# A first tile that is finished in PSUM, and a second MoE whose second layer streams tokens instead of weights

## The chip, the cores and the metric

One program runs on one NeuronCore of a Trainium2 chip. Its engines work beside each other and wait for one another through semaphores: TensorE (PE, matrix products into PSUM, which has eight banks of 512 fp32 a partition), VectorE (DVE), ScalarE (ACT), GpSimd (POOL) and SyncE (SP, which here only starts DMAs). The metric is device microseconds (us) of one execution, as the median of several; lower is better.

## The reference, cut to what matters

```python
# delta attention: q, k, v of shape (4, 8, 768, 48), one 48x48 state per head
for t in range(S):
    y[:, :, t] = q_t @ state
    state = state + bt * outer(kt, vt - kt @ state)
x = y.transpose(0, 2, 1, 3).reshape(3072, 384)
# first MoE: 384 -> 2048 -> 384
h = x @ w_in
x = (h * sigmoid(1.702 * h)) @ w_out
# second MoE: 4 experts, 384 -> 1024 -> 384
p = domain_probs / (domain_probs.sum(-1) + 1e-9)
out = sum(p[:, e:e+1] * (np.maximum(x @ w1[e], 0) @ w2[e]) for e in range(4))
```

Everything is fp32. A product of the MoEs is done as three products of parts: each operand is split into a high part and the rest, and high x high, high x rest and rest x high are added in PSUM (`PASSES`).

## The kernel before, in words

The 768 positions are twelve chunks of 64, called u = 0 to 11. Two chunks of all four batches are one tile of 512 tokens, so there are six tiles, t = 0 to 5.

**Attention.** For each chunk a chain of small fp32 products runs over the heads (each leaves two records in the trace): Gram matrices of the keys (L511, L514), products of keys and queries (L444), for u = 0 and 1 two more that complete an inverse (L661, L670), keys times state (L733), solves (L743, twice), a cross term (L753), the output `y` (function `read`, L765) and the state update (`write`, L770). Chunks 0 and 1 are worked in two halves of the heads, one after the other. `y` comes out with one head pair's 48 rows on partitions 0 to 47 and another's on 64 to 111. For the first MoE the 384 features must lie on 128 partitions in three parts, so `y_copy` moves three heads of four into the tile `stage` and the fourth into a side buffer `YS`, and six DMAs of 16 rows (`put`, L848) bring the pieces of the fourth head into the 16 free partitions under each 48. Then `split_stage` splits `stage` into the two parts that the MoE takes (`xs`, L180 and L878).

**First MoE.** A visit f of 16 takes 128 hidden features: nine products into `ph` (function `layer1`, L884: three parts of x, three passes), the gate on ACT and DVE, and nine products into the three `px` banks (L972) that are issued a visit late. In both layers the weights are loaded into the array and 512 tokens stream through it. Tile 0 does its first eight visits on 256 tokens of u = 0, then on 256 tokens of u = 1, then eight on all 512; tile 1 is worked in halves throughout. The weights of tile 0's visits are themselves split into parts on ACT and DVE shortly before they are used (`queue_w1`, L262 to L277).

**What sets the order.** `manual_schedule` keeps instructions as they are written. `Order` writes attention tasks into the stream of MoE products by a cost model with clocks, priorities and ready times; `until` moves its clock on until a task is done. Each engine then runs its own list in order, so a product that waits holds all later products.

**Second MoE.** For each expert e and tile t, eight visits f. Layer 1 is as before. ACT and DVE make the two parts of the hidden tile, `hh` (L1112, L1113). In `layer2_2` (L1086) the hidden tile is loaded into the array, 128 tokens at a time, and 384 columns of weights stream: twelve products for the four groups of tokens. After the eighth visit DVE scales each `po` bank by the tokens' probability and adds it to `oacc` (L1092, L1094); after the last expert a DMA writes each 128 tokens out (L1098). The part of x for the next tile is split during the visit before the last (L1077, L1078); the first one is split when the first MoE is over. The weights of the next expert are split in the last tile of an expert.

Of the kernel before, what the change touches and what calls it, by code (L numbers as in the profile page):

```python
# [149 lines left out]
def delta_attention_moe_moe_kernel(  # L150
# [17 lines left out]
    E = probs.shape[1]  # L168
    F2 = we.shape[0] // E
# [52 lines left out]

    def load_w2(n):
        nc.sync.dma_start(out=raw[:, n % 2, :], in_=we[n])

    def split_w2(n):
        t = wp.tile([128, 2, 768], F32R, name="w", tag="w")
        half = raw[:, n % 2, :]
# [94 lines left out]
    V = nc.vector  # L323

# [98 lines left out]
    def queue_q(u):  # L423
# [11 lines left out]
        for g0 in range(0, NP, 8):  # L435
            cell = {}

            def gram(g0=g0, cell=cell):
                ps = cell["ps"] = psa.tile([128, 8, C], F32, name="gp", tag=claim(BANKS, cell["end"]))
                for i in range(8):  # L440
                    g = g0 + i
                    for x in range(2):
                        d = DR[x]
                        mm(ps[TR[x]:TR[x] + C, i, :], lhsT=kt[d:d + D, g, :], rhs=pq[d:d + D, g, x, :],  # L444
                           start=True, stop=True)

            def mask(x, g0=g0, cell=cell):
                r = TR[x]
                V.tensor_tensor(out=pq[r:r + C, g0:g0 + 8, x, :], in0=cell["ps"][r:r + C],  # L449
                                in1=pmask[r:r + C].unsqueeze(1).broadcast_to([C, 8, C]), op=ALU.mult)  # L450

            visits.append(gram)
            masks += [(cell, lambda x=x, mask=mask: mask(x)) for x in range(2)]
            if len(visits) == whole:
                t = task(lambda fs=tuple(visits): [f() for f in fs], "PE", 1.0 * whole,
                         (*placed[u], lq, begun[0], *ends[-1:]), prio=p + 1, can=lambda: some_free(BANKS, whole))
                for c, f in masks:
                    c.setdefault("end", []).append(task(f, "DVE", 0.6, (t,), prio=p + 1))
                    ends.append(c["end"][-1])
                visits.clear()  # L460
                masks.clear()
# [225 lines left out]
    def queue_chain(u):  # L687
# [27 lines left out]
        for hu in range(2):  # L715
# [65 lines left out]
            def s_add(x, gs=gs, cell=cell):  # L781
# [4 lines left out]
                else:  # L786
# [3 lines left out]
                               read=read, write=write, y_copy=y_copy, s_add=s_add))  # L790


        for hs in [halves[0:1], halves[1:2]] if u < 2 else [halves]:
# [29 lines left out]
            if n == 1:  # L823
                h, = hs
                reads = [task(h["read"], "PE", 1.0, (*bs, pdone[u]), prio=p, can=lambda: free_at("yg"))]
# [4 lines left out]
            for h, y in zip(hs, reads):  # L830
                ye = h["cell"]["yev"] = [task(lambda e, x=x, h=h: h["y_copy"](e, x), ("ACT", "DVE"), (0.7, 0.72), (y,), prio=p,
                                              can=y_free) for x in range(2)]
                wr = task(h["write"], "PE", 0.82, bs, prio=p) if n == 1 else reads[0]
# [7 lines left out]


        ov = []
        for x in range(2):
            for kk in range(KD):
                def put(x=x, kk=kk):
                    d, n = DR[x] + 16 * kk, DR[x] + D
                    (nc.scalar if u < 2 and x else nc.sync).dma_start(out=xst[n:n + 16, kk, u % 2], in_=YS[u][d:d + 16])  # L848

                ov.append(task(put, "ACT" if u < 2 and x else "HW", 0.45, yev, lat=2.3, prio=p, slack=5))  # L850
# [5 lines left out]
    xst = stage.rearrange("p (k c b i) -> p k c b i", k=KD, b=B, c=2)  # L856

# [31 lines left out]
    with tc.manual_schedule():  # L889
# [6 lines left out]
        nc.gpsimd.memset(SU, 0.0)  # L896
        m2 = scr[2][:, 0:C]
# [33 lines left out]
        x1 = {}  # L931
        x1d = [drx.tile([128, KD, TT], F32, name=f"x1d{t}") for t in range(KEEP)]
# [4 lines left out]
        def queue_w2(n):  # L937
            e, f = divmod(n, F2)
            WE[e, f] = split_w2(n)
            if n + 2 < E * F2:  # L940
                load_w2(n + 2)

        def x1_out(t):
# [16 lines left out]
            return ev  # L960

# [44 lines left out]
        def split_stage(t, cs, us, fs):  # L1006
            if not us:
                return split
            until(*(ydone[u] for u in us))
            if cs.start == 0:  # L1010
# [10 lines left out]
        for n, (t, cs, us, fs) in enumerate(items):  # L1021
            if cs.start == 0 and fs[0] == 0 and t + 2 < NW:
                queue_tile(t + 2)
            for f in fs:
# [17 lines left out]
                if t == NW - 1 and 1 <= f <= F2:  # L1042
                    queue_w2(f - 1)
                if t == NW - 1 and f == F1 // 2:
                    nc.vector.tensor_reduce(out=ptmp, in_=pr, axis=mybir.AxisListType.X, op=ALU.add)
                    nc.vector.tensor_scalar(out=ptmp, in0=ptmp, scalar1=1e-9, scalar2=None, op0=ALU.add)
                    nc.vector.reciprocal(out=ptmp, in_=ptmp)
                    nc.vector.tensor_tensor(out=pr, in0=pr, in1=ptmp.unsqueeze(3).broadcast_to([128, B, NW, E]), op=ALU.mult)
            if t == NW - 2:
# [8 lines left out]
                oacc = big.tile([128, B, NW, DM], F32, name="oacc")  # L1058
                pr = big.tile([128, B, NW, E], F32, name="pr")
                ptmp = big.tile([128, B, NW], F32, name="ptmp")  # L1060
# [4 lines left out]
                nc.sync.dma_start(out=pr, in_=probs.rearrange("(b t p) e -> p b t e", b=B, p=128))  # L1065
# [8 lines left out]
        def split_now(n, t, kk):  # L1074
            s = (xs2 if n % 2 else xsp).tile([128, 2, TT], F32R, name="xs", tag="xs")
            src = x1[t][:, kk, :]
            nc.scalar.copy(out=s[:, 0, :], in_=src)  # L1077
            nc.vector.tensor_tensor(out=s[:, 1, :], in0=src, in1=s[:, 0, :].bitcast(F32), op=ALU.subtract)  # L1078
            return s

        def layer2_2(e, t, f, hh, w):
            for b in range(B):
                if f == 0:
                    po[b] = ps2.tile([128, DM], F32, name="po", tag="po", bufs=6)
                for i, (a, c) in enumerate(PASSES):
                    mm(po[b], lhsT=hh[:, a, b * 128:(b + 1) * 128], rhs=w[:, c, 384:768],  # L1086
                       start=f == 0 and i == 0, stop=f == F2 - 1 and i == 2)
                if f == F2 - 1:
                    acc = oacc[:, b, t, :]
                    p = pr[:, b, t, e:e + 1]  # L1090
                    if e == 0:
                        nc.vector.tensor_scalar(out=acc, in0=po[b], scalar1=p, scalar2=None, op0=ALU.mult)  # L1092
                    else:
                        nc.vector.scalar_tensor_tensor(out=acc, in0=po[b], scalar=p, in1=acc,  # L1094
                                                       op0=ALU.mult, op1=ALU.add)
                    if e == E - 1:
                        r0 = b * S + t * 128
                        nc.sync.dma_start(out=out[r0:r0 + 128, :], in_=acc)  # L1098
# [3 lines left out]
        xs = [split_now(0, 0, kk) for kk in range(KD)]  # L1102
        for n, (e, t) in enumerate(seq):
            nt = seq[n + 1][1] if n + 1 < len(seq) else None
            for f in range(F2):
# [9 lines left out]
                if pend:  # L1115
                    layer2_2(*pend)
# [5 lines left out]
            if e + 1 < E and t == NW - 1:  # L1122
                queue_w2((e + 1) * F2 + F2 - 1)
        layer2_2(*pend)


def lay_out(q, k, v, beta, moe_w_in, moe_w_out, moe2_domain_probs, moe2_w1, moe2_w2):
# [13 lines left out]

    qt = flat(q.reshape(B, M, 2, U, C, D).transpose(3, 2, 5, 0, 1, 4), U, 2, D, B * M, C)
# [12 lines left out]
    for kk in range(KD):  # L1155
        for x in range(2):
# [4 lines left out]
    we = np.concatenate([flat(w1, -1, 128, DM), moe2_w2.reshape(-1, 128, DM)], axis=2)  # L1161
    return {"q": qt, "k": tokens(k), "v": tokens(v), "beta": betas, "w": w,
            "probs": np.ascontiguousarray(moe2_domain_probs), "we": we}
# [20 lines left out]
```

## Time and profile before

| | us |
|---|---|
| median of three runs | 1480.54 (1479.08 to 1483.88) |
| the profiled execution | 1484.33 |
| its span, first to last instruction | 1482.6 |
| PE busy | 1420.4 (96% of the span) |
| DVE busy | 619.3 (42%) |
| ACT busy | 459.8 (31%) |
| POOL busy | 191.9 (13%) |

The span has four parts: attention ahead of any MoE (to 86.55 us), the first tiles, in which attention and the first MoE share PE, the first MoE alone, and from 676.30 us the second MoE. PE counts as busy while a product is anywhere in its pipeline, so a busy PE isn't at its peak: a row of the timeline gives when a run of products starts, and the distance from one start to the next is what the run takes. An engine's idle time counts only where PE waits for it.

### The profile page before, as it was taken

What the parts mean: (1) busy time and instruction counts of PE and PEld (TensorE: products, weight loads), DVE (VectorE), ACT (ScalarE), POOL (GpSimd) and SP (SyncE); (2) the same over time, 40 slices, a digit from 0 to 9 for tenths busy, and PEclk for the clock granted to TensorE, in tenths of its full rate; (3) what the DMA queues carried; (4) which work ended last, traced back from release to release, by engine and by line L of the source; (5) the groups of instructions that cost most, each with busy time, mean ns of one, the idle gap of its engine ahead of it and who ended that gap; (6) DMA issues with size and microseconds to landing.
All of it is one profiled execution on the core that took longest, in us unless ns stands there. A gap on an engine that the chain in (4) does not pass through costs nothing.

```text
span 1482.6 us, 30388 instructions
## 1 busy us (share of the span) xinstructions
PE 1420.4 (96%) x13552; PEld 1258.2 (85%) x13552; DVE 619.3 (42%) x1033; ACT 459.8 (31%) x866; POOL 191.9 (13%) x340
## 2 busy tenths in 40 slices
PE   3687999999999999999999999999999999999999
PEld 2677889998888788888999999999999999999998
DVE  6978756545473423332223242232433223423222
ACT  5554434445353233432111231121321112222111
POOL 2019550080260530000000000000000000000000
PEclk8588999999999999999999999999999999999999
DMA  9211021201201000410000020000200000100001
GB/s 316 115 27 36 2 74 34 62 22 26 49 23 37 15 33 8 142 52 1 0 1 0 10 77 0 1 0 1 64 22 0 1 0 22 43 22 22 22 22 43
DMA packets 41331, 53.71 MB, mean 36 GB/s; under 512 B 25712, under 2 KB 29936, under 8 KB 41200
## 3 DMA queue, kind: packets, MB, share of 16 engines
q1 hardware_dynamic: 41008, 51.67, 11.7%
q8 instruction: 106, 1.74, 0.5%
q14 instruction: 25, 0.20, 0.0%
q10 hardware_dynamic: 192, 0.10, 0.0%
HBM read 42.71 MB, written 7.86 MB: 34 GB/s over the span
## 4 chain that ended last, share of the span: by engine, by line
PE 90%; DVE 2%; DMA 1%; ACT 1%; SPq 0%; issue 0%; DVEq 0%
PE ph L884 40%; PE po L1086 27%; PE px L972 13%; PE ch L743 2%; PE gp L444 2%; PE ch L733 1%; PE y L765 1%; DMA pq<-in_q_dram 1%; PE ch L753 1%; PE ch L770 1%; PE gp L511 1%; SPq L848 0%; DVE w L277 0%; DVE gh L990 0%; DVE scr L479 0%
## 5 line engine op out<-in xcount | busy, mean ns | idle before, releaser
L884 PE MATMUL ph<-xs,w 128*128 128x512 f32 (+1 forms) x2808 | 664.8, 379 | 3.7 <-DVE x L180 2.4
L884 PEld LDWEIGHTS ph<-xs,w 128*128 128x128 f32 x2808 | 499.7, 190 | 90.3 <-issue 2.8
L1086 PE MATMUL po<-w,hh 128*128 128x384 f32 x2304 | 432.8, 336 | 0.0
L1086 PEld LDWEIGHTS po<-w,hh 128*128 128x128 f32 x2304 | 407.6, 188 | 17.1
L1113 DVE SCALAR_TENSOR_TENSOR hh<-ph,hh 128x512 fp32r<-128x512 f32 x192 | 132.9, 692 | 554.0 <-ACT hh L1112 554.0
L1112 ACT ACTIVATE hh<-ph 128x512 fp32r<-128x512 f32 x192 | 115.0, 599 | 632.3 <-PE ph L884 632.3
L972 PE MATMUL px<-gh,w 128*128 128x512 f32 (+1 forms) x1080 | 233.5, 356 | 0.6 <-DVE gh L990 0.4
L972 PEld LDWEIGHTS px<-gh,w 128*128 128x128 f32 x1080 | 178.5, 192 | 29.4 <-DVE gh L990 2.0
L990 DVE TENSOR_TENSOR gh<-ph,gh 128x512 fp32r<-128x512 f32 (+1 forms) x120 | 69.5, 579 | 147.7 <-ACT gh L989 146.9
L987 ACT ACTIVATE ph<-ph 128x512 f32<-128x512 f32 (+1 forms) x120 | 59.5, 496 | 207.8 <-PE ph L884 203.5
L569 POOL TENSOR_TENSOR scr<-scr,itmp 128x30 f32<-128x30 f32 (+9 forms) x150 | 89.4, 596 | 11.8
L567 POOL TENSOR_TENSOR itmp<-scr 128x30 f32<-128x30 f32 (+9 forms) x150 | 81.4, 543 | 11.4
L989 ACT CAST gh<-ph 128x512 fp32r<-128x512 f32 (+1 forms) x120 | 60.2, 502 | 3.8
L180 ACT COPY su<-ch 32x384 f32<-32x384 f32 x77 | 36.2, 471 | 49.6 <-PE ch L743 45.0
L444 PE MATMUL gp<-pq,kt 48*64 48x64 f32 x768 | 34.2, 254 | 18.1 <-DMA pq<-in_q_dram 9.5
L444 PEld LDWEIGHTS gp<-pq,kt 48*64 48x64 f32 x768 | 31.3, 166 | 21.4 <-issue 8.3
L1078 DVE TENSOR_TENSOR xs<-x,xs 128x512 fp32r<-128x512 f32 x72 | 45.3, 684 | 2.0 <-ACT xs L1077 2.0
L511 PE MATMUL gp<-kt 48*32 48x64 f32 x768 | 28.2, 231 | 17.0 <-ACT kt L180 16.2
L743 PEld LDWEIGHTS ch<-v,scr 32*32 32x32 f32 x1536 | 36.5, 110 | 7.8 <-issue 4.6
L511 PEld LDWEIGHTS gp<-kt 48*32 48x32 f32 x768 | 25.2, 116 | 20.8 <-ACT kt L180 17.6
L743 PE MATMUL ch<-v,scr 32*32 32x48 f32 x1536 | 40.4, 208 | 0.7 <-DVE pq L449 0.5
L180 ACT COPY kt<-scr 32x512 f32<-32x512 f32 (+1 forms) x60 | 37.0, 617 | 12.0 <-DVE scr L333 11.1
(106 smaller groups left out, 809.6 us busy)
## 6 DMA issues: line engine op xcount, KB each, us to landing
raw<-in_we_dram SPq DMA_DIRECT2D x32, 384.0 KB, 3.1
rw<-in_w_dram SPq DMA_DIRECT2D x14, 768.0 KB, 12.2
k<-in_k_dram SPq DMA_DIRECT2D x12, 384.0 KB, 5.1
pq<-in_q_dram SPq DMA_DIRECT2D x24, 192.0 KB, 4.5
v<-in_v_dram SPq DMA_DIRECT2D x12, 384.0 KB, 3.2
out_dram<-oacc SPq DMA_DIRECT2D x24, 192.0 KB, 1.9
x1d<-raw SPq DMA_DIRECT2D x12, 256.0 KB, 2.3
x<-x1d SPq DMA_DIRECT2D x4, 768.0 KB, 5.8
```

The costliest lines, as they stand in the source:

```text
L180: (nc.scalar.copy if e == "ACT" else nc.vector.tensor_copy)(out=out_, in_=in_)
L444: mm(ps[TR[x]:TR[x] + C, i, :], lhsT=kt[d:d + D, g, :], rhs=pq[d:d + D, g, x, :], start=True, stop=True)
L511: mm(ps[r:r + SB, i, :], lhsT=kt[d:d + D, g, 0:SB], rhs=kt[d:d + D, g, :], start=True, stop=True)
L567: E.tensor_tensor(out=tv, in0=x[:, j:j + 1, j + 1:].broadcast_to([128, m, r]), in1=x[:, 0:m, j:j + 1].broadcast_to([128, m, r]), op=ALU.mult)
L569: E.tensor_tensor(out=x[:, 0:m, j + 1:], in0=x[:, 0:m, j + 1:], in1=tv, op=ALU.add)
L743: mm(cell["ps"][r:r + 32, i, :], lhsT=Tb[u][r:r + 32, g, :], rhs=V2[u][r:r + 32, g, :], start=True, stop=True, tile_position=(r, r))
L884: mm(ps, lhsT=w[:, a, kk * 128:(kk + 1) * 128], rhs=xs[kk][:, b, cs], start=kk == 0 and i == 0, stop=kk == KD - 1 and i == 2)
L972: mm(px[d][:, cs], lhsT=w[:, a, 384 + d * 128:384 + (d + 1) * 128], rhs=gh[:, b, 0:cs.stop - cs.start], start=f == 0 and i == 0 and cs.sta ...
L990: a = task(lambda: nc.vector.tensor_tensor(out=lo, in0=ph, in1=hi.bitcast(F32), op=ALU.subtract), "DVE", 0.07 + 0.53 * c, (a,), **kw)
L1086: mm(po[b], lhsT=hh[:, a, b * 128:(b + 1) * 128], rhs=w[:, c, 384:768], start=f == 0 and i == 0, stop=f == F2 - 1 and i == 2)
L1112: nc.scalar.activation(out=hh[:, 0, :], in_=ph, func=AF.Relu)
L1113: nc.vector.scalar_tensor_tensor(out=hh[:, 1, :], in0=ph, scalar=0.0, in1=hh[:, 0, :].bitcast(F32), op0=ALU.max, op1=ALU.subtract)
```

## The change

Three things are changed, and some tables around them.

**First tile.** For u = 0 and 1, `read` no longer makes the fourth head's outputs as 48 rows of their own. `S4`, a view of `stage`, is set to zero at the start on POOL; `fourth` copies the fourth head's 16 columns for each part beside zeros, so that a product with 64 columns of it puts them on rows 48 to 63 and zeros on the rows above, and the three-head product is added on top. The finished 128 rows are split straight from PSUM by `take_x` and `take_rest` into `xs0`. The copies, the six DMAs and `split_stage` are gone for tile 0. `write` now follows its half's `read`, and key and query products of u above 1 may only be placed once the first MoE has begun.

**Second MoE, layer 2.** In tiles 0 to 4 the weights are loaded and the 512 tokens of `hh` stream, into three banks of 128 features. The probabilities lie along the tokens then: they are normalised once, written to a DRAM buffer `prd`, and loaded per expert and tile, broadcast to all partitions, into half of `raw` (`load_pb`). DVE multiplies each bank by them and adds it. After the last expert DVE transposes blocks of 32x32 and sixteen DMAs write the tile out. The last tile keeps the old form (`layer2_last`), with its weight columns read in another order, since `lay_out` permutes them on the host. The next expert's weights are split in tiles 1 to 4, two a tile.

**First x of the second MoE.** `split_now(0, 0, kk)` is called four visits before the end of the first MoE.

```diff
-                    mm(py[o:o + D, i, :], lhsT=SU[:, c0:c0 + D], rhs=pq[:, g, x, :], start=True, stop=True)
+                    if not t and g % 4 == KD:
+                        continue
+                    if not t:
+                        g3 = g - g % 4 + KD
+                        mm(py[o:o + C, i, :], lhsT=S4[:, g // 4, x, g % 4, :], rhs=pq[:, g3, x, :], start=True, stop=False)
+                    mm(py[o:o + D, i, :], lhsT=SU[:, c0:c0 + D], rhs=pq[:, g, x, :], start=bool(t), stop=True)
+            def fourth(e, hu=hu):
+                copy(e, S4[:, bs, :, :, D:].rearrange("p b x k i -> p (b x k) i"),
+                     SU[:, 0:NP * 2 * D].rearrange("p (b m y) -> p b m y", b=B, m=4)[:, bs, KD, :])
+            def take_x(e, kk, hu=hu, cell=cell):
+                copy(e, xs0[kk][:, 0, c0:c0 + TT // 4].rearrange("p (b i) -> p b i", i=C),
+                     cell["py"].rearrange("p (b m) i -> p m b i", m=4)[:, kk])
+            def take_rest(kk, hu=hu, cell=cell):
+                V.tensor_tensor(out=lo, in0=cell["py"].rearrange("p (b m) i -> p m b i", m=4)[:, kk], in1=hi.bitcast(F32),
+                                op=ALU.subtract)
...
+        nc.gpsimd.memset(stage, 0.0)
...
-                         (*placed[u], lq, begun[0], *ends[-1:]), prio=p + 1, can=lambda: some_free(BANKS, whole))
+                         (*placed[u], lq, begun[0], *ends[-1:]), prio=p + 1,
+                         can=lambda: None if u > 1 and not od.moe else some_free(BANKS, whole))
...
+                bs.append(task(h["fourth"], ("ACT", "DVE"), (0.35, 0.35), bs, prio=p))
...
-                wr = task(h["write"], "PE", 0.82, bs, prio=p) if n == 1 else reads[0]
+                wr = task(h["write"], "PE", 0.82, (y,), prio=p) if n == 1 else reads[0]
...
+                if t == NW - 1 and f == F1 - 4:
+                    first = [split_now(0, 0, kk) for kk in range(KD)]
...
         def layer2_2(e, t, f, hh, w):
-            for b in range(B):
+            for kk in range(KD):
                 for i, (a, c) in enumerate(PASSES):
-                    mm(po[b], lhsT=hh[:, a, b * 128:(b + 1) * 128], rhs=w[:, c, 384:768],
+                    mm(po[kk], lhsT=w[:, a, 384 + kk * 128:384 + (kk + 1) * 128], rhs=hh[:, c, :],
                        start=f == 0 and i == 0, stop=f == F2 - 1 and i == 2)
+                if f == F2 - 1:
+                    nc.vector.tensor_tensor(out=ps, in0=ps, in1=pb[e, t], op=ALU.mult)
+                    nc.vector.tensor_tensor(out=acc[:, kk], in0=acc[:, kk], in1=ps.rearrange("p (c j) -> p c j", j=32),
+                                            op=ALU.add)
+            if f == F2 - 1 and e == E - 1:
+                for h in range(2):
+                    nc.vector.transpose(out=half, in_=half)
+                for b in range(B):
+                    for a in range(4):
+                        r0 = b * S + t * 128
+                        nc.sync.dma_start(
+                            out=out[r0:r0 + 128, a * 96:(a + 1) * 96].rearrange("(q j) d -> j q d", j=32),
+                            in_=oacc[t][a * 32:(a + 1) * 32, b * DM:(b + 1) * DM].rearrange("j (q d) -> j q d", q=4))
+        def layer2_last(e, t, f, hh, w):
+                    mm(ps, lhsT=hh[:, a, b * 128:(b + 1) * 128],
+                       rhs=w[:, c, 384:768].rearrange("p (k a i) -> p a k i", a=4, k=KD),
...
-                if e + 1 < E and t == NW - 1 and f >= 1:
-                    queue_w2((e + 1) * F2 + f - 1)
+                if f == 1 and n:
+                    load_pb(n)
+                if e + 1 < E and 1 <= t <= F2 // 2 and f in (2, 4):
+                    queue_w2((e + 1) * F2 + (t - 1) * 2 + f // 2 - 1)
```

PE around the end of u = 1's outputs (`y`), first in the kernel before (a product of L765 is `y`, of L770 the state update, of L444 the query product of u = 3, of L884 the first layer, of L972 the second):

```order
L770 MATMUL ch_1390<-su,k_1_82 48x48 x16
L770 MATMUL ch_1314<-su,k_1_82 48x48 x16
L765 MATMUL y<-pq_79,su 48x64 x16
L444 MATMUL gp<-pq_79,kt_77 64x64 x32
L884 MATMUL ph<-xs,w 128x256 x9
L972 MATMUL px_1193<-gh,w 128x256 x3
```

The same place on PE after the change, where the lines are numbered anew: L799 is the state update, L931 the first layer, L1029 the second, L450 the query product:

```order
L799 MATMUL ch_1310<-su,k_1_82 48x48 x16
L931 MATMUL ph<-xs,w 128x256 x9
L1029 MATMUL px_1017<-gh,w 128x256 x3
L1029 MATMUL px_1018<-gh,w 128x256 x3
L1029 MATMUL px_1019<-gh,w 128x256 x3
L931 MATMUL ph<-xs,w 128x256 x9
L1029 MATMUL px_1017<-gh,w 128x256 x3
L1029 MATMUL px_1018<-gh,w 128x256 x3
L1029 MATMUL px_1019<-gh,w 128x256 x3
L931 MATMUL ph<-xs,w 128x256 x6
L450 MATMUL gp<-pq_79,kt_77 64x64 x32
```

The query product of u = 3 has moved from ahead of the first visit of this half to behind the first layer of its third; that of u = 2 has moved in the same way, from ahead of all visits to between u = 1's two reads.

PE in the second MoE, two visits of the kernel before:

```order
L884 MATMUL ph_8339<-xs,w 128x512 x9
L1086 MATMUL po<-w,hh 128x384 x12
L884 MATMUL ph_8368<-xs,w 128x512 x9
L1086 MATMUL po<-w,hh 128x384 x12
L884 MATMUL ph_8393<-xs,w 128x512 x9
L1086 MATMUL po<-w,hh 128x384 x12
```

PE after the change, where the turned form (L1156) passes into the old one (L1186) at the last tile:

```order
L931 MATMUL ph_13046<-xs,w 128x512 x9
L1156 MATMUL po<-hh,w 128x512 x9
L931 MATMUL ph_13092<-xs,w 128x512 x9
L1186 MATMUL po<-w,hh 128x384 x12
L931 MATMUL ph_13121<-xs,w 128x512 x9
L1186 MATMUL po<-w,hh 128x384 x12
```

In tiles 0 to 4 twelve products of 384 columns have become nine of 512.

DVE at a tile's end under the last expert, before (L1113 is the rest of `hh`, L1094 the weighted sum):

```order
L1113 SCALAR_TENSOR_TENSOR hh<-ph_13190,hh 128x512
L1094 SCALAR_TENSOR_TENSOR oacc<-po,pr,oacc 128x384 x4
L1113 SCALAR_TENSOR_TENSOR hh<-ph_13223,hh 128x512
L1113 SCALAR_TENSOR_TENSOR hh<-ph_13252,hh 128x512
L1113 SCALAR_TENSOR_TENSOR hh<-ph_13277,hh 128x512
```

And after (L1217 is the rest of `hh`, L1164 the product with the probabilities, L1165 the sum, L1170 the transposes):

```order
L1217 SCALAR_TENSOR_TENSOR hh<-ph_12833,hh 128x512
L1164 TENSOR_TENSOR po<-po,raw 128x512
L1165 TENSOR_TENSOR oacc_7904<-oacc_7904,po 128x16x32
L1164 TENSOR_TENSOR po<-po,raw 128x512
L1165 TENSOR_TENSOR oacc_7904<-oacc_7904,po 128x16x32
L1164 TENSOR_TENSOR po<-po,raw 128x512
L1165 TENSOR_TENSOR oacc_7904<-oacc_7904,po 128x16x32
L1170 STREAM_TRANSPOSE oacc_7904<-oacc_7904 128x768 x2
L1217 SCALAR_TENSOR_TENSOR hh<-ph_12879,hh 128x512
```

Four operations have become six, and under the last expert eight; they stand between the same two visits.

## Rows read from the trace of the kernel before

**Rows 1.** The page: busy time, share of the span and instructions by engine.

```profile
PE 1420.4 (96%) x13552; PEld 1258.2 (85%) x13552; DVE 619.3 (42%) x1033; ACT 459.8 (31%) x866; POOL 191.9 (13%) x340
```

**Rows 2.** Chain in order of time, second MoE: start us, us, what.

```profile
707.88 2.09 PE ph L884 x9
...
774.76 2.09 PE ph L884 x9
```

**Rows 3.** Timeline of PE, first MoE: start us, us, what, count.

```profile
643.05 2.20 PE L884 MATMUL ph<-xs,w 128*128 128x512 f32 x9
645.09 2.20 PE L972 MATMUL px<-gh,w 128*128 128x512 f32 x9
...
667.53 2.20 PE L884 MATMUL ph<-xs,w 128*128 128x512 f32 x9
```

**Rows 4.** Timeline of PE, runs of 256 columns.

```profile
137.69 1.24 PE L884 MATMUL ph<-xs,w 128*128 128x256 f32 x9
138.77 1.24 PE L972 MATMUL px<-gh,w 128*128 128x256 f32 x9
```

**Rows 5.** Timeline of PE, second MoE.

```profile
707.72 2.25 PE L884 MATMUL ph<-xs,w 128*128 128x512 f32 x9
709.81 2.24 PE L1086 MATMUL po<-w,hh 128*128 128x384 f32 x12
```

**Rows 6.** Timeline of PE, first MoE, behind a run of small products.

```profile
161.69 2.11 PE L884 MATMUL ph<-xs,w 128*128 128x512 f32 x8
163.63 2.20 PE L972 MATMUL px<-gh,w 128*128 128x512 f32 x9
```

**Rows 7.** Groups by line and shape: busy us, mean ns, idle before.

```profile
L1113 DVE SCALAR_TENSOR_TENSOR hh<-ph,hh 128x512 fp32r<-128x512 f32 x192 | 132.9, 692 | 554.0 <-ACT hh L1112 554.0
L333 DVE STREAM_TRANSPOSE scr<-k 128x512 f32<-128x512 f32 x24 | 16.0, 694 | 0.3
L590 DVE STREAM_TRANSPOSE scr<-scr 128x1024 f32<-128x1024 f32 x6 | 13.1, 2177 | 0.0
```

**Rows 8.** Timeline, where the second MoE begins; in brackets the idle time before.

```profile
673.00 1.66 ACT L1077 CAST xs<-x 128x512 fp32r<-128x512 f32 x3
...
675.47 0.68 DVE L180 COPY x<-px 128x512 f32<-128x512 f32 x1
676.30 4.36 PE L884 MATMUL ph<-xs,w 128*128 128x512 f32 x18 [2.43 <-DVE x L180]
```

**Rows 9.** Timeline, first tile, u = 0's outputs and the first visit.

```profile
61.13 1.95 PE L765 MATMUL y<-pq,su 128*48 128x64 f32 x32
...
80.79 0.40 ACT L180 CAST xs<-stage 128x256 fp32r<-128x256 f32 x1
...
82.94 3.67 PE L444 MATMUL gp<-pq,kt 48*64 48x64 f32 x62 [0.86 <-DMA pq<-in_q_dram]
...
86.55 4.21 PE L884 MATMUL ph<-xs,w 128*128 128x256 f32 x18
```

**Rows 10.** Timeline of PE, first tile, u = 1's outputs, its half's first visits, and the first 512-wide one.

```profile
118.56 1.10 PE L765 MATMUL y<-pq,su 128*48 128x64 f32 x32
...
127.94 3.67 PE L444 MATMUL gp<-pq,kt 48*64 48x64 f32 x62 [1.03 <-DMA pq<-in_q_dram]
131.55 2.29 PE L884 MATMUL ph<-xs,w 128*128 128x256 f32 x9
...
151.75 2.23 PE L884 MATMUL ph<-xs,w 128*128 128x512 f32 x9
```

**Rows 11.** Timeline of PE: u = 2's last outputs, tile 1's first visit, an undisturbed query product.

```profile
193.76 1.10 PE L765 MATMUL y<-pq,su 128*48 128x64 f32 x32
...
205.17 1.34 PE L884 MATMUL ph<-xs,w 128*128 128x256 f32 x9
...
225.81 2.15 PE L444 MATMUL gp<-pq,kt 48*64 48x64 f32 x62 [0.99 <-DMA pq<-in_q_dram]
```

**Rows 12.** Timeline of DVE: the last weights of the first MoE are split.

```profile
146.13 0.94 DVE L277 TENSOR_TENSOR w<-raw,w 128x768 fp32r<-128x768 f32 x1
```

More of the change, by code (lines that the diff above doesn't have):

```diff
@@ L168, in delta_attention_moe_moe_kernel @@
     E = probs.shape[1]
+    NP_ = probs.shape[2]
     F2 = we.shape[0] // E
@@ L323, in delta_attention_moe_moe_kernel @@
     V = nc.vector
+    xs0 = [xsp.tile([128, 2, TT], F32R, name="xs", tag="xs") for _ in range(KD)]
+    direct = {}
     def queue_turn(u, k2t, deps, p):
@@ L840, in queue_chain @@
         edone[u] = task(lambda: None, None, 0.0, ends, lat=0.0, prio=p)
+        if not t:
+            direct[u] = yev
+            ydone[u] = task(lambda: None, None, 0.0, yev, lat=0.0, prio=p)
+            return
         ov = []
@@ L847, in put @@
                     d, n = DR[x] + 16 * kk, DR[x] + D
-                    (nc.scalar if u < 2 and x else nc.sync).dma_start(out=xst[n:n + 16, kk, u % 2], in_=YS[u][d:d + 16])
-                ov.append(task(put, "ACT" if u < 2 and x else "HW", 0.45, yev, lat=2.3, prio=p, slack=5))
+                    nc.sync.dma_start(out=xst[n:n + 16, kk, u % 2], in_=YS[u][d:d + 16])
+                ov.append(task(put, "HW", 0.45, yev, lat=2.3, prio=p, slack=5))
         whole["end"] = ov
@@ L960, in x1_out, with split_now @@
             return ev
+        def split_now(n, t, kk):
+            s = (xsp if n % 2 else xs2).tile([128, 2, TT], F32R, name="xs", tag="xs")
+            src = x1[t][:, kk, :]
+            nc.scalar.copy(out=s[:, 0, :], in_=src)
+            nc.vector.tensor_tensor(out=s[:, 1, :], in0=src, in1=s[:, 0, :].bitcast(F32), op=ALU.subtract)
+            return s
         evac = []
@@ L1009, in split_stage @@
             until(*(ydone[u] for u in us))
+            if not t:
+                xs[:] = xs0
+                return [a for u in us for a in direct[u]]
             if cs.start == 0:
@@ L1072, in delta_attention_moe_moe_kernel, with load_pb @@
         po = {}
[L1074 to L1079, printed above, removed]
-        def layer2_2(e, t, f, hh, w):
+        pb = {}
+        def load_pb(n):
+            e, t = seq[n]
+            if t == NW - 1:
+                return
+            pb[e, t] = raw[:, 1, 0:TT]
+            nc.sync.dma_start(out=pb[e, t], in_=prd[e:e + 1, t * TT:(t + 1) * TT].broadcast_to([128, TT]))
@@ L1097, in layer2_2 @@
                         r0 = b * S + t * 128
-                        nc.sync.dma_start(out=out[r0:r0 + 128, :], in_=acc)
+                        nc.sync.dma_start(out=out[r0:r0 + 128, :], in_=acc[:, b])
         pend = None
         seq = [(e, t) for e in range(E) for t in range(NW)]
-        xs = [split_now(0, 0, kk) for kk in range(KD)]
+        load_pb(0)
+        pr5 = big.tile([128, E, B], F32, name="pr5")
+        for e in range(E):
+            nc.sync.dma_start(out=pr5[:, e], in_=prd[e, (NW - 1) * TT:].rearrange("(b p) -> p b", b=B))
+        xs = first
         for n, (e, t) in enumerate(seq):
@@ L1140, in tokens @@
         return flat(a, U, 2 * C, B * M * D)
+    N = B * S
+    tiles = lambda a: a.reshape(B, N // B // 128, 128, -1).transpose(3, 1, 0, 2)
     qt = flat(q.reshape(B, M, 2, U, C, D).transpose(3, 2, 5, 0, 1, 4), U, 2, D, B * M, C)
```

83 lines of the change are left out of this document (58 added, 25 removed).

## The prediction

> **What bounds the kernel now.** I read the page's busy times first: PE has 96% of the span, so a gain must be shorter PE work or a PE wait that goes [rows 1]. Then the chain in order of time for the second MoE: sixteen visits from 707.88 to 774.76, 66.88 us or 4.18 each, hold nothing but PE, so this half is bound by the rate of products [rows 2]. The timeline shows each visit as two runs, 2.09 us of nine products and 2.09 of twelve [rows 5]. The first MoE alone, where both layers stream 512 tokens, takes 24.48 us for the six visits from 643.05 to 667.53, or 4.08, and 2.04 for the first run of nine there [rows 3]. Last I read the timeline for PE's stops: one where the second MoE begins [rows 8], and in the first tile one ahead of each half's first visit [rows 9, 10]. Attention and tile 0 are not PE's alone: PE waits there for the query DMA that a product in its list needs, and the x of a half passes through copies, DMAs and a split.
>
> **Layer 2 of the second MoE.** In five of six tiles under four experts, 4 x 5 x 8 = 160 of 192 visits, 12 x 384 columns become 9 x 512: 4608 either way. What can change is the cost of a product beyond its columns. Nine of 256 take 138.77 - 137.69 = 1.08 us, 120 ns each [rows 4]; nine of 512 take 2.04, 227 each [rows 3]. So 256 columns cost 107 ns and a product some 13 ns more. Three products fewer are then worth 3 x 13.3 = 0.04 us a visit. But the visit after the change has the shape that the first MoE has already, nine and nine of 512, and that takes 4.08 where the present one takes 4.18. The remaining 0.06 is, I think, a cost of changing between long and short products: the run of eight that follows a run of small products at 161.69 takes 163.63 - 161.69 = 1.94, 242 ns each and not 227 [rows 6], and here the nine of 512 take 2.09 behind products of 384 where they take 2.04 behind their like [rows 3, 5]. I take the like-shaped row: 0.10 x 160 = **16.0 us**. The low bound is the fixed cost alone, 0.04 x 160 = 6.4. Below it lies nothing saved, if columns alone decide.
>
> The Trainium skill speaks for that last case: "TensorE: Matmul & The Clock Gate", section "Back-to-back issue gap", gives N/2.4 + 2.5 ns for a product by itself. By that figure three products fewer would be an estimated 3 x 2.5 ns x 160 = 1.2 us. The trace disagrees with it as a price here: 4.18 against 4.08 for the same 9216 columns [rows 2, 3].
>
> DVE pays for the turn. At a tile's end it has six operations where it had four, at 0.69 each by a 512-wide one [rows 7]. Let E be the end of the last visit's layer 2. The banks finish one after another, so the six end near E + 3.45, and the rest of the next hidden tile, queued behind them on DVE, at E + 4.1. Layer 2 needs it after three PE runs of 2.04, at E + 6.1: no wait. Under the last expert two transposes of 768 come in between. A transpose of 512 takes 694 ns, so 1.04 each [rows 7]; the rest is then ready near E + 6.1, just in time. At the rate of L590's (2177 ns for 1024 [rows 7]) they take 1.63 each, and five tiles lose about 1 us each, 5 at most. I take nothing. The broadcast load (256 KB), the weights split in tiles 1 to 4 and sixteen output DMAs a tile have 33 us of PE work over them; without that cover a load would stop PE as the query's does below, in the 8.3 us from 119.66 to 127.94 [rows 10]. The last tile keeps its form, so the tail stays.
>
> **First x of the second MoE.** PE waits 2.43 us before 676.30, and the last move of `x` out of `px` on DVE releases it [rows 8]. Beside it ACT makes the first x's three high parts for 1.66, between the last evictions. Moved ahead, these and DVE's three rests (0.69 each by rows 7, 2.1) can spread over four visits of 4.08 [rows 3]. The last gate work isn't then behind them, so the moves end a cast run sooner: **1.6 us**. The other 0.8 is the moves themselves. Bounds: 0, if the moves are late for another reason, and 2.4.
>
> **First tile.** `fourth` costs the side that copies 0.4 by a cast of 256 [rows 9], beside other work. Each `read` has 48 records instead of 32; at 1.95/32 = 61 ns [rows 9] that is 1.0 us more on PE a half for u = 0, half that where products go at u = 1's rate (1.10 for 32 [rows 10]). What goes are the copies, six DMAs and the split from `stage`; in their place come six short operations from PSUM a half. From 61.13 I add: read 2.9, state update 1.0, the other half's the same, half a Gram matrix 1.0, which gives 70. The last cast (0.40 [rows 9]) and rest end beside it near 72. The first visit begins at **72** for 86.55 [rows 9]. That is 14.5 us, but not yet gain: the inverse's products for u = 1 (3.0), the rest of the Gram matrices (1.0) and the query product of u = 2 (2.15 [rows 11]) now stand among the visits instead of ahead of them, and the extra records cost 1.1. PE works in the meantime, so u = 1's outputs end near 110 for 119.66, and since the x comes straight from PSUM and the query product of u = 3 (with the stop ahead of it, to 127.94, and 3.67 of its own [rows 10]) stands behind the third visit, the half's first visit is at **114** for 131.55: 17 earlier.
>
> Now the weights come late. DVE makes their last rest at 146.13 to 147.07 [rows 12], for a visit of 512 at 151.75 [rows 10]. DVE has lost its part of tile 0's copies and split, but its chain of weights is otherwise as long, and PE now comes sooner. I put the 512-wide visits at **137** (133 to 142), so 14.5 of the 17 are left. Two more of them, 8.2 us, stand ahead of u = 2's chain. Its outputs, at 193.76 before [rows 11], come near 185, and go by copies, DMAs and split as before: 205.17 - 194.86 = 10.3 us from their end to tile 1 [rows 11]. Before, PE work covered most of this; now about 4 us does, and some 5 us of idle come anew. Tile 1 begins at **194** for 205.17. Of these 11 us, PE work left over behind that point takes 1.7, and a slow stretch after the new idle some 2: L444 takes 3.67 behind a stop and 2.15 without it [rows 10, 11]. **7 us** is left. Bounds: 2, if the weights bind until 142, and 12, if work is found for the idle. Zeroing `stage` on POOL lies at the start, 60 us ahead of its first use [rows 9]; if something behind it on POOL or its queue is late by it, that comes off the low bound.
>
> **Sum.** 16.0 + 1.6 + 7 = 24.6. The profiled execution is 1484.33 us, 1.73 outside its span of 1482.6, so 1459.7; against the median, 1480.54 - 24.6 = **1456**. Its own range takes 12 to 18 of the turn, 0 to 2.4 of the entry, 2 to 12 of the tile: 1448 to 1465.
>
> **Rivals.** A: only the fixed cost of three products goes, and the surcharge stays since rows 6 come from another place: 6.4 + 1.6 + 7 = 15.0, 1465.5. For it: one row for the cause. Against it: the like-shaped visit takes 4.08 over six visits. Chance 0.12. With columns alone deciding, the turn gives 0 to 1.2 and the total is 1471; chance 0.05, since it contradicts rows 2 and 3. B: the first tile gives nothing, because weights bind to 147 and the idle ahead of tile 1 is the whole 10.3: 16.0 + 1.6 = 17.6, 1463. Chance 0.09. C, slower: the last tile's weights are read as runs of 32 floats, 128 apart, in 4 x 8 x 12 = 384 products. No row shows such an operand. If it streams at half rate, 384 columns cost 160 ns more each [rows 3, 4], 61 us, and the time is 1517. It decides from 24.6/384 = 64 ns, over a third of the present 174 [rows 5]. The attention's strided operands show nothing of the sort, though none is this wide. Chance 0.03. D: the DVE work at the tile's end holds PE for 1 us under the last expert, and as much at each of the other 15 borders: 20 x 1 = 20, which leaves 1476. Against it stand 2 us of slack at those 15. Chance 0.03.
>
> **How the numbers follow.** Forecast 0.68. The range should hold A's and B's times and leave the column rule, C and D out with the edges: 1447 to 1468. Faster by over 0.3% (4.4 us, about what can be told from no change) are the forecast, A, B, the column case and half of D: 0.95; same 0.02, slower 0.03.
>
> **What would show it.** Turned visits start 4.08 apart, the last tile's 4.18; 4.14 speaks for A. PE enters the second MoE after less than 1 us idle. First visit near 72, the second half's near 114, the first of 512 near 137, tile 1 near 194 with 5 us idle ahead. Products of the last tile much over 174 ns show C, a wait for the rest of `hh` behind a border D. The forecast is wrong by most if 16.0 isn't there: then the visits' spacing tells it at once.

## The result, and the profile after

The changed kernel takes 1468.29 us (median of four, 1464.18 to 1470.51) for 1481.52 of the kernel before: a ratio of 0.9909, interval 0.9888 to 0.9930. That is 13.2 us (10 to 17) for the 24.6 forecast, and 0.3 us above the upper end of the range. The profiled execution has a span of 1468.8 us, 13.8 less than before.

The page's busy times: microseconds, share of the span, instructions.

```profile
PE 1416.0 (96%) x13136; PEld 1195.9 (81%) x13136; DVE 648.4 (44%) x1067; ACT 457.7 (31%) x867; POOL 191.6 (13%) x341
```

PE still bounds the kernel, as in [rows 1]. The timeline at the entry of the second MoE (start us, us, engine, line; in brackets the idle time before):

```profile
668.09 0.69 DVE L181 COPY x<-px 128x512 f32<-128x512 f32 x1 [2.19 <-PE px L1029]
668.88 4.43 PE L931 MATMUL ph<-xs,w 128*128 128x512 f32 x18 [0.83 <-ACT x L181]
```

The second MoE begins at 668.88 for 676.30, after 0.83 us of idle and not 2.43 [rows 8]: 1.6 of the 13.8 are the entry's, 5.8 lie ahead of it. The second MoE takes 1468.8 - 668.9 = 799.9 us for 806.3, which is the other 6.4, and there the forecast had 16. The chain in order of time shows what became of them. First the border between tiles 2 and 3 of the first expert, then the last tile (L931 is the first layer, L1156 the turned second, L1186 the old form):

```profile
762.37 2.10 PE ph L931 x9
764.47 2.08 PE po L1156 x9
766.55 2.04 PE ph L931 x9
768.59 2.04 PE po L1156 x9
...
836.71 2.04 PE ph L931 x9
838.75 2.15 PE po L1186 x12
```

Up to 766.55 a visit takes 2.10 + 2.08 = 4.18, as before the change [rows 5]; from there on it takes 4.08, as in the first MoE [rows 3]. It changes at a tile's first product and holds for eight visits. Over all experts tiles 1 and 3 run at 4.08, tiles 0, 2 and 4 at 4.18, and the last tile, in the old form with strided columns, at 2.04 + 2.15 = 4.19. So 4 x 2 x 8 = 64 visits gained 0.10, 6.4 us, and 96 gained nothing.

In the first tile PE's first visits came where the forecast put them or sooner. Timeline of PE: the first visits of u = 0, the second read of u = 1 with a stop ahead of it, the first visits of u = 1's half and of 512 columns, u = 2's last outputs, and the first visits of tile 1; then the windows around them (stretch in us, PE busy, granted clock as a share of full speed, DMA share, GB/s):

```profile
69.88 2.28 PE L931 MATMUL ph<-xs,w 128*128 128x256 f32 x17 [0.58 <-DVE xs L793]
...
109.76 0.34 PE L776 MATMUL y<-pq,stage 128*64 128x64 f32 x4 [2.98 <-DVE pq L455]
...
112.15 1.55 PE L931 MATMUL ph<-xs,w 128*128 128x256 f32 x9
...
133.95 2.23 PE L931 MATMUL ph<-xs,w 128*128 128x512 f32 x9
...
185.65 1.10 PE L777 MATMUL y<-pq,su 128*48 128x64 f32 x32
...
189.53 1.83 PE L740 MATMUL ch<-su,kt 48*64 48x48 f32 x32 [1.59 <-DVE su L813]
...
193.99 0.58 PE L931 MATMUL ph<-xs,w 128*128 128x256 f32 x1
195.00 2.07 PE L931 MATMUL ph<-xs,w 128*128 128x256 f32 x8 [0.43 <-DVE xs L925]
```

```profile
188.00:192.00 4.00, 2.47 (x50) 0.71 0.11 30
192.00:196.00 4.00, 3.57 (x57) 0.50 0.72 115
196.00:200.00 4.00, 4.00 (x71) 0.50 0.37 95
200.00:204.00 4.00, 4.00 (x56) 0.58 0.00 0
```

Tile 1 begins at 194 for 205.17 [rows 11], 11 us earlier, behind 1.59 + 0.43 = 2.0 us of idle. But from about 190 PE runs at half the full clock (1.2 GHz), behind the stop of 1.59 ahead of tile 1. Of 16 us there, up to 0.29 x 4 + 0.50 x 4 + 0.50 x 4 + 0.42 x 4 = 6.8 are lost. The kernel before has a granted clock of 1.00 in every window from 136 to 224 us.

### The profile page after: what moved, and what is told of

Read it like the earlier page. It is cut to its first block, busy times and chain, and to the rows that moved or that the text cites. A ratio compares the mean times of both kernels' runs of the same rounds, so it can differ in the third digit from the quotient of the medians.

```text
span 1468.8 us, 29677 instructions
## 1 busy us (share of the span) xinstructions
PE 1416.0 (96%) x13136; PEld 1195.9 (81%) x13136; DVE 648.4 (44%) x1067; ACT 457.7 (31%) x867; POOL 191.6 (13%) x341
## 3 DMA queue, kind: packets, MB, share of 16 engines
q1 hardware_dynamic: 52032, 56.88, 13.2%
## 4 chain that ended last, share of the span: by engine, by line
PE 89%; DVE 4%; issue 1%; DMA 1%; SPq 0%; ACT 0%; DVEq 0%
PE ph L931 40%; PE po L1156 22%; PE px L1029 13%; PE po L1186 5%; PE ch L750 2%; PE y L777 2%; PE ch L740 1%; PE ch L760 1%; PE ch L799 1%; PE gp L450 1%; PE gp L518 1%; DVE w L281 1%; DMA pq<-in_q_dram 0%; DVE kt L181 0%; DVE gh L1047 0%
## 5 line engine op out<-in xcount | busy, mean ns | idle before, releaser
L931 PE MATMUL ph<-xs,w 128*128 128x512 f32 (+1 forms) x2808 | 660.7, 377 | 3.4 <-DVE xs L925 1.6
L931 PEld LDWEIGHTS ph<-xs,w 128*128 128x128 f32 x2808 | 500.8, 189 | 101.8 <-DVE xs L925 2.4
L1217 DVE SCALAR_TENSOR_TENSOR hh<-ph,hh 128x512 fp32r<-128x512 f32 x192 | 132.6, 690 | 512.6 <-ACT hh L1216 512.6
L1156 PE MATMUL po<-hh,w 128*128 128x512 f32 x1440 | 355.9, 391 | 0.0
L1156 PEld LDWEIGHTS po<-hh,w 128*128 128x128 f32 x1440 | 270.4, 188 | 60.4
L1029 PE MATMUL px<-gh,w 128*128 128x512 f32 (+1 forms) x1080 | 234.0, 356 | 1.6 <-DVE gh L1047 1.1
L1029 PEld LDWEIGHTS px<-gh,w 128*128 128x128 f32 x1080 | 178.5, 192 | 31.2 <-DVE gh L1047 2.7
L1186 PE MATMUL po<-w,hh 128*128 128x384 f32 x384 | 73.9, 342 | 0.0
L1186 PEld LDWEIGHTS po<-w,hh 128*128 128x128 f32 x384 | 69.3, 188 | 2.5
```

The lines of the kernel that those rows point to most:

```text
L931: mm(ps, lhsT=w[:, a, kk * 128:(kk + 1) * 128], rhs=xs[kk][:, b, cs], start=kk == 0 and i == 0, stop=kk == KD - 1 and i == 2)
L1029: mm(px[d][:, cs], lhsT=w[:, a, 384 + d * 128:384 + (d + 1) * 128], rhs=gh[:, b, 0:cs.stop - cs.start], start=f == 0 and i == 0 and cs.sta ...
L1156: mm(po[kk], lhsT=w[:, a, 384 + kk * 128:384 + (kk + 1) * 128], rhs=hh[:, c, :], start=f == 0 and i == 0, stop=f == F2 - 1 and i == 2)
L1186: mm(ps, lhsT=hh[:, a, b * 128:(b + 1) * 128], rhs=w[:, c, 384:768].rearrange("p (k a i) -> p a k i", a=4, k=KD), start=f == 0 and i == 0, ...
L1217: nc.vector.scalar_tensor_tensor(out=hh[:, 1, :], in0=ph, scalar=0.0, in1=hh[:, 0, :].bitcast(F32), op0=ALU.max, op1=ALU.subtract)
```

## The experiments

A visit's two rates were the first question. What differs between tiles 1, 3 and tiles 0, 2, 4 is the buffer of x: two pools take turns (`xsp` and `xs2`), and the program's memory map has them at bytes 120992 and 215744 of a partition. The weights start at 22688 and the hidden tile at 133280. Counted from a multiple of 256 bytes, `xs2` lies at 192, and `xsp`, the weights and the hidden tile at 160.

### e1: the second buffer of x at another place

```diff
                 xs2 = ctx.enter_context(tc.tile_pool(name="xs2", bufs=3))
+                small = ctx.enter_context(tc.tile_pool(name="small", bufs=1))
-                pr = big.tile([128, E, NP_], F32, name="pr")
+                pr = small.tile([128, E, NP_], F32, name="pr")
...
```

> The changed kernel with the three small tiles pr, ptmp and pr5 put behind the second buffer of x instead of ahead of it; nothing else moves. In the trace after the change the turned visits take 4.08 us in tiles 1 and 3 and 4.18 in tiles 0, 2 and 4, and these differ by the buffer that x lies in. That buffer of tiles 0, 2 and 4 starts at byte 215744 of a partition (704 past a multiple of 2048), the other at 120992 and the hidden tile at 133280 (both 160 past one). Here it starts at 215200, 160 past one too. Theory A (the place of x decides the rate): all turned visits 4.08, 96 x 0.10 = 9.6 us less, 1458.7. Theory N (something else tells the tiles apart: the order of their work, their PSUM banks): still 4.18 in three tiles, 1468.

1457.53 us (1454.60 to 1462.53), ratio to the kernel before 0.9843 (0.9818 to 0.9869), 10.8 us below the changed kernel. The chain in a tile 2 (L1157 is the turned layer):

```profile
739.80 2.04 PE po L1157 x9
741.84 2.04 PE ph L931 x9
```

All turned visits take 4.08. The place of x decides; theory N has fallen. The gain is the 9.6 expected, within the interval; the second MoE alone takes 790.7 us for 799.9 after the change.

### e2, e3, e5, e6, e12: how large the unit is

Five more places for `xs2`, each by a pad ahead of it (e2's is shown, the others differ in its length), in e2 and e3 from the changed kernel, in the others from e1:

```diff
+        big.tile([128, 8], F32, name="pad")
```

> The changed kernel with a pad of 32 bytes ahead of the second buffer of x: it starts at 215776, which is 32 past a multiple of 64, as the other x and the hidden tile are, but 736 past a multiple of 2048. Theory A with a small unit (where in 64 bytes a row begins): all turned visits 4.08, 1458.7. Theory A with a large unit (where in 1024 or 2048 bytes): 4.18 in tiles 0, 2 and 4, 1468. Theory N: 1468.

> The changed kernel with a pad of 480 bytes ahead of the second buffer of x: it starts at 216224, 32 past a multiple of 64, 160 past a multiple of 1024 but 1184 past one of 2048. Theory A with a unit of 64 or of 1024: turned visits 4.08 in all tiles, 1458.7. With a unit of 2048: 4.18 in tiles 0, 2 and 4, 1468. Theory N: 1468.

> The kernel with the small tiles behind the second buffer of x, and 512 bytes of pad ahead of it: it starts at 215712, 160 past a multiple of 512 but 672 past one of 1024. The runs so far: 4.08 us in all turned visits with the start at 160 past a multiple of 1024, 4.18 in three tiles with 704 or 736. If the unit is 1024: tiles 0, 2 and 4 are back near 4.18 (1467). If it is 512 or a part of it: 4.08 everywhere (1457.5).

> As the kernel before it, with 256 bytes of pad: the second buffer of x starts at 215456, 160 past a multiple of 256 but 416 past one of 512. Unit of 256 or less: 4.08 everywhere (1457.5). Unit of 512 or more: tiles 0, 2 and 4 near 4.18 (1467).

> The kernel of e1_behind with 128 bytes of pad ahead of the second buffer of x: it starts at 215328, 32 past a multiple of 128, as the other x does, but 32 and not 160 past one of 256. The pads of 256 and 512 left 4.08 everywhere. Unit 128: 4.08 everywhere, 1457. Unit 256: tiles 0, 2 and 4 near 4.18, 1467.

The chain in tile 2, of e2, then of e12, then of e6:

```profile
735.11 2.06 PE ph L931 x9
737.17 2.09 PE po L1156 x9
```

```profile
736.26 2.07 PE po L1158 x9
738.33 2.09 PE ph L931 x9
```

```profile
736.74 2.04 PE po L1158 x9
738.78 2.04 PE ph L931 x9
```

| kernel | start of `xs2` | past a multiple of 256 | visit in tiles 0, 2, 4 | us |
|---|---|---|---|---|
| after | 215744 | 192 | 2.10 + 2.08 | 1468.29 |
| e2 | 215776 | 224 | 2.06 + 2.09 | 1467.81 |
| e12 | 215328 | 32 | 2.09 + 2.07 | 1469.81 (one run) |
| e1 | 215200 | 160 | 2.04 + 2.04 | 1457.53 |
| e6 | 215456 | 160 | 2.04 + 2.04 | 1463.56 (one run) |
| e5 | 215712 | 160 | 2.04 + 2.04 | 1459.01 (one run) |
| e3 | 216224 | 160 | 2.04 + 2.04 | 1460.21 |

Three places at 160 past a multiple of 256 beside e1's give the full rate, and 192, 224 and 32 don't. The second MoE by itself shows it free of what varies ahead of it: 790.7 us in each of e1, e3, e5 and e6, but 797.1 in e2, 798.0 in e12 and 799.9 after the change. (e6's whole time holds a stretch of low clock early on, 0.50 to 0.55 in the windows from 84 to 104 us.) By e2 a unit of 64 is out, by e12 one of 128, by e6 one above 256. The expectation of e6 had allowed 512 and more, which fell. That the operands need only agree, and not lie at 160 itself, wasn't tried.

### e7 and e11: whether a change between 512 and 384 columns costs

e7 is the kernel before, with x of every second tile moved from 640 to 672 past a multiple of 1024 (from 128 to 160 past one of 256):

```diff
+                big.tile([128, 8], F32, name="pad")
                 oacc = big.tile([128, B, NW, DM], F32, name="oacc")
```

> The kernel before, whose second layer streams weights that start 672 past a multiple of 1024, with 32 bytes of pad ahead of the second buffer of x: that starts at 215712, 672 past a multiple of 1024 too, where it was at 640. Every second tile of the second MoE takes its x from there. Theory A: in these tiles the nine products of 512 go from 232 ns to 227, a visit from 4.18 to near 4.13, and 96 visits give some 5 us, 1477. Theory S (the change between products of 512 and of 384 columns costs, as the forecast had it): 4.18 stays, 1481.5.

e11 is e1's kernel with the last tile's weight columns read in a row:

```diff
-                       rhs=w[:, c, 384:768].rearrange("p (k a i) -> p a k i", a=4, k=KD),
+                       rhs=w[:, c, 384:768],
```

> The kernel of e1_behind whose last tile reads 384 weight columns in a row instead of in runs of 32; its columns of that tile come out in another order. In the strided form a product takes 180 ns and the products of 512 beside it 227, a visit 4.19. Theory S (a change between products of 512 and 384 columns costs where they lie in phase): products near 175 and 231, as in the kernel before, a visit 4.18, nothing gained: 1457. If all that the kernel before lost had been the place of x: 173 and 227, a visit 4.12, 32 x 0.07 = 2 us less.

The chain in a moved tile of e7, then in the last tile of e11:

```profile
712.56 2.10 PE po L1087 x12
714.67 2.08 PE ph L884 x9
```

```profile
851.74 2.10 PE po L1187 x12
853.85 2.08 PE ph L931 x9
```

With x, the weights and the hidden tile all at 160 past a multiple of 256, a visit of 9 x 512 and 12 x 384 still takes 4.18 to 4.19, in both kernels. So theory A has fallen for the old form, and theory S's price is there. Its reason, the change of length, isn't shown. In the last tile of e1 the lengths change too, and there the nine of 512 take 2.04; it is the twelve strided ones that take 2.15, and the visit 4.19. Nor is the cost paid where the length changes: by the starts of single products in e7, all nine of 512 are spaced 224 to 236 ns, as with a displaced x, and of the twelve the first six 171 to 185 and the others 173 to 174. What in the old form costs it stays open. e7's one time, 1484.16, is 0.4 above the highest of the kernel before (1477.36 to 1483.79, median 1480.36 over 13 runs): nothing was gained. e11's, 1476.31, can't be compared: the granted clock was 0.50 from 84 to 116 us in it, for 1.00 in the changed kernel. Two windows of e11:

```profile
84.00:88.00 4.00, 4.00 (x86) 0.51 0.02 4
...
112.00:116.00 4.00, 4.00 (x58) 0.50 0.02 6
```

### e4 and e8: the two halves of the change alone

e4 leaves the first tile as it was, e8 the second MoE and the entry.

> The kernel before with the turned second layer and the first x split ahead, and without the change of the first tile. By the trace after the change these are worth 6.4 and 1.6 us: 1481.5 - 8.0 = 1473.5, second MoE 0.8 us after the last eviction and 800 us long. If the first tile's 5.8 us in that trace were a difference between two executions only, it would come out at 1468 as the whole change does.

> The kernel before with the change of the first tile alone. By the trace after the change the first MoE ends 5.8 us earlier: 1475.7. By the forecast 7: 1474.5. With the turn alone at 9.5 below the kernel before, and the whole change at 13.2, some 3.7 are left for it: 1477.8.

The timeline where the second MoE begins, of e4 and of e8:

```profile
670.60 4.43 PE L888 MATMUL ph<-xs,w 128*128 128x512 f32 x18 [0.83 <-ACT x L181]
```

```profile
669.14 5.97 PE L927 MATMUL ph<-xs,w 128*128 128x512 f32 x18 [2.44 <-DVE x L180]
```

e4 takes 1472.19, ratio 0.9941 (0.9926 to 0.9956): 9.5 us less than the kernel before beside it, for 8.0 expected. The idle time is 0.83 with the split ahead and 2.44 without it, so the entry's 1.6 is shown from both sides. It can be worth more: in e8 and e7 the first eighteen products behind the stop of 2.44 take 5.97 us, where they take 4.36 in the kernel before [rows 8] and 4.43 after the change. The clock was low there in e8 and not in the profile of before, by a window of each:

```profile
668.00:672.00 4.00, 2.86 (x7) 0.67 0.00 0
```

```profile
676.00:680.00 4.00, 3.70 (x16) 1.00 0.01 4
```

e8 takes 1479.14 for 1480.36, ratio 0.9998 (0.9978 to 1.0018), where 1474.5 to 1477.8 was expected, and scatters from 1475.67 to 1486.98: by itself the first tile's change can't be told from nothing.

Yet e8 reaches the second MoE at 669.14, 7.2 us ahead of the profile of before. Part of that is the profiled execution's own. e7 has no change ahead of the second MoE and reaches it at 673.11, 3.2 earlier than the profile of before does. Windows of before:

```profile
494.00:498.00 4.00, 2.55 (x53) 0.92 0.08 11
498.00:502.00 4.00, 4.00 (x30) 0.66 0.00 0
```

That execution had a stop of 1.45 us near 495 and a low clock behind it, 3 us in all; e4, e7 and e8 don't have it, nor has the profile after. What the first tile gives is then 5.8 - 3.2 = 2.6 in the profile after and 7.2 - 3.2 = 4.0 in e8's. Both hang on single executions. After, e1, e2, e3, e5, e6, e9 and e12 have the same products up to the second MoE, and reach it anywhere from 663.01 (e3) to 671.17 us (e6), 668.0 in the mean; without the first tile's change, and with the entry's 1.6 taken off where it isn't, it is 674.7 (before), 671.5 (e7) and 670.6 (e4), 672.3 in the mean. That makes some 4 us, by an estimate from few executions. The difference between the whole change and e4, 0.9909 to 0.9941, 4.7 us, has an interval that holds both.

### e9 and e10: where the first tile's lead goes

e10 puts products with no use into the gaps of PE ahead of tile 1; e9 is e1's kernel, on the same chip.

```diff
+            def hold(n):
+                ps = psh.tile([128, TT], F32, name="ph", tag="ph")
+                for _ in range(n):
+                    mm(ps, lhsT=W[0][:, 0, 0:128], rhs=W[0][:, 0, 0:TT], start=True, stop=True)
...
+                    return lambda: [hs[0][name](*args), hold(8), hs[1][name](*args), hold(4)]
+                return lambda: [*(h[name](*args) for h in hs), hold(10)]
```

> The kernel of e1_behind once more, on the chip of the next one, as its base: 1457.5 (1454.6 to 1462.5 there). Its executions should differ by how long PE stays at the low clock around the begin of tile 1, 6.8 to 12 us lost in the traces so far.

> The kernel of e1_behind with 22 products of 512 columns on weights, whose sums nobody reads, put into the gaps ahead of tile 1 (8, 4 and 10 of them, 227 ns each, 5 us at full clock). They do no work of the reference. Theory C (the clock takes back what the first tile gains: after the new stop near 188 us the trace shows a granted clock of 0.50 for 12 to 20 us, 6.8 to 12 us lost): the clock stays up, tile 1's first visit begins near 194 as before, its later visits 6 to 10 us earlier, 1450. Theory D (it is lost to DVE and DMA that the visits of tile 1 wait for, the clock only follows): the visits after it stay where they are, 1457 to 1460, with the products' own time on top.

Windows of e9, then of e10:

```profile
192.00:196.00 4.00, 3.61 (x82) 0.59 0.10 25
196.00:200.00 4.00, 3.10 (x29) 0.50 0.86 146
200.00:204.00 4.00, 4.00 (x69) 0.50 0.20 63
204.00:208.00 4.00, 4.00 (x71) 0.70 0.00 0
```

```profile
192.00:196.00 4.00, 4.00 (x77) 1.00 0.73 125
196.00:200.00 4.00, 4.00 (x81) 1.00 0.33 88
...
216.00:220.00 4.00, 2.67 (x22) 1.00 0.88 140
220.00:224.00 4.00, 2.99 (x56) 0.56 0.20 57
224.00:228.00 4.00, 4.00 (x30) 0.58 0.00 0
```

e10 takes 1457.86 (0.9846, 0.9822 to 0.9870), e9 1460.96 (0.9875, 0.9850 to 0.9900): 3 us, with intervals that overlap. The clock stays up where it fell, which by these windows had cost up to 6.8 us in e9; theory C holds for the mechanism, but not for its 1450 us. The lead comes to the next stop instead. The query products behind tile 1's first visits and the next ones, of e9, then of e10:

```profile
217.32 2.08 PE L450 MATMUL gp<-pq,kt 48*64 48x64 f32 x64
...
225.46 2.08 PE L450 MATMUL gp<-pq,kt 48*64 48x64 f32 x62 [0.81 <-DMA pq<-in_q_dram]
```

```profile
211.28 2.08 PE L450 MATMUL gp<-pq,kt 48*64 48x64 f32 x64
...
221.01 3.67 PE L450 MATMUL gp<-pq,kt 48*64 48x64 f32 x62 [1.31 <-DMA pq<-in_q_dram]
```

e10 is 6.0 us ahead at the first. Then it waits 1.03 + 1.31 us for a query DMA, where e9 waits 0.81, and the clock falls there in e10 alone (up to 3.4 us lost in the last two windows); the second MoE begins 1.65 us earlier, at 665.70 for 667.35. The 22 products also take 5 us of PE, more than the gaps they fill. Of theory D that much is true: a lead at tile 1 is handed on to the next thing that is late. e1 (1457.53, and 1460.96 as e9) and e10 (1457.86) have the lowest medians here, below both kernels that were compared.

## Why the prediction was right or wrong

**What bounds.** Right: PE's rate in the second MoE, and PE's stops in the first tile.

**Layer 2.** The 0.10 us a visit was right as the price of the old form. Of its two parts, the 13 ns a product fits the 173 to 174 ns of the later products of 384 in e7 (160 for the columns and 13); the other 0.06 is there with everything in phase (e7, e11), but that it is a cost of changing length isn't shown. The step that failed is "I take the like-shaped row", for all 160 visits. The row of 4.08 was measured where every operand lies at the same place in 256 bytes; the second MoE takes every second x from a pool that doesn't. A like shape was not a like case. The old form paid 4.17 to 4.19 in both pools, so in tiles 0, 2 and 4 one cost took the place of the other, and 16.0 became 6.4. With the pool moved (e1), 16.0 is there (the second MoE takes 806.3 - 790.7 = 15.6 less than before), and 1457.53 beside the 1456 forecast; that the total comes so near is in part luck, as the first tile gave less than its 7. Rival A had the price, 6.4, and the wrong reason: it expected 4.14 in all tiles. The column rule fell. By the figure of the Trainium skill, "TensorE: Matmul & The Clock Gate", section "Back-to-back issue gap", the two forms of a visit would lie an estimated 8 ns apart; the trace disagrees, with 0.10 us where the operands agree (e7, e1).

**DVE at a tile's border.** Right. Under the last expert the transposes take 957 ns for the 1.04 us estimated, and the rest of the hidden tile comes in time: its last part starts at 1405.61 and takes 0.65, and the layer that reads it starts at 1406.66, right behind the run of nine from 1404.56. That leaves 0.4 us to spare. Timeline of DVE and PE there:

```profile
1403.85 1.84 DVE L1170 STREAM_TRANSPOSE oacc<-oacc 128x768 f32<-128x768 f32 x2
1404.56 2.26 PE L931 MATMUL ph<-xs,w 128*128 128x512 f32 x9
...
1405.61 0.65 DVE L1217 SCALAR_TENSOR_TENSOR hh<-ph,hh 128x512 fp32r<-128x512 f32 x1
...
1406.66 2.24 PE L1156 MATMUL po<-hh,w 128*128 128x512 f32 x9
```

Rival D didn't come. Nor did C: strided columns cost 180 - 173 ns a product and not 160, and the runs of nine beside them took 2.04 for 2.08, which gave most of it back.

**The entry.** 1.6 of idle, as forecast. The low clock that can follow the longer stop (1.6 more in e7 and e8) wasn't in the sum.

**First tile.** The places came as forecast or sooner: first visit at 69 to 70 for 72, the second half's at 112 for 114, the first of 512 columns at 134 for 137, tile 1 at 194 for 194. That is in part luck, since two places of the chain don't follow from its terms. With 14.5 us won and 3.0 + 1.0 + 2.15 + 1.1 put among the visits, u = 1's outputs would end at 112.4 and not near 110, and with 8.2 for two visits u = 2's would begin at 187.5 and not near 185. The trace has 111.4, with a stop of 2.98 us between u = 1's two reads that the forecast didn't have, and 185.65. Low clock that went helped: it is 1.00 in the windows from 64 to 156 us, where the kernel before has 0.50 at 84 to 88 and 124 to 132. The idle ahead of tile 1 was 2.0 for the 5 forecast. The term that was mis-sized is "a slow stretch after the new idle some 2": it took up to 6.8 in the profile after, and a second one near 224 took 3.4 where the kernel before lost 1.7 (0.96 and 0.61 in its windows from 224 to 232), together 8.5 more than before. So of 11 us of lead, 7 were to stay and 2.6 did, or some 4 over all executions. Rival B's direction was right, but its cause (late weights) wasn't: the first visits of 512 came sooner than forecast. The profiled execution of before also held 3 us of its own, near 495, as its place above all three runs shown could have told.

**The sum.** 6.4 + 1.6 + 2.6 to 4.0 = 10.6 to 12.0, for 13.2 measured, with an interval of 10 to 17. The least that the prediction's own bounds allow, 12 + 0 + 2 = 14, gives 1466.5 and not the 1465 that it states; its final range reached to 1468 all the same.

## What to carry to other kernels

A row of the same shape prices an operation only if its operands lie alike in memory; before a pool or a small tile is added, look where it moves the moving operands, and compare the rate buffer by buffer. Time won ahead of a wait is won only if the wait doesn't grow: a stop that opens on TensorE costs its own length and can cost a stretch at half clock behind it, which ahead of tile 1 took more than the stop (up to 6.8 us for 2.0). And take a stage's length from more than one profiled execution when a term is a few microseconds.

## What the runs showed of the hardware

The place of the streamed operand within 256 bytes sets a rate: at 160 like the other operands a product of 512 columns follows the last after 227 ns, at 192, 224 or 32 after 229 to 233 in the mean. The second layer's products slow down in the same tiles, 231 ns at 192, although their own operands haven't moved; why they do stays open. In the changed kernel the pattern of spacings repeats within a nanosecond from visit to visit. The slow-down follows the neighbour: the last visit's second layer in a slow tile, which runs beside the next tile's x, is back at 227.

The granted clock early in the program is a matter of the execution. With PE at work in both, it was 1.00 from 84 to 92 us in the profile after and 0.50 in e11, for over 30 us there. The kernels with the changed first tile scatter more (6 to 11 us from the lowest time to the highest) than the kernel before (4 to 6) and e4 (2.5), and this is the likely reason; only the profiled executions show their clock over time, so it is argued and not shown. A stop of the same length doesn't always bring the clock down: behind the 2.43 and 2.44 us at the entry it was 1.00 in the kernel before, 0.67 in e8's window and 0.65 in e7's.
